# Dense layer with seven products: sums on VectorE, another PSUM bank for the second part, a later fourth part, three buffers for narrowed weights

## Chip, cores and metric

The kernel runs on one core of a Trainium2 chip. The metric is the device time of one execution in microseconds (us); three executions of the kernel before are shown.

## What is computed

The reference has three stages: an attention whose weights are sigmoids, an expert layer with one of eight experts per token, and a dense layer. The change touches the dense layer and the weights that are prepared for it. It is, for 1792 tokens, `d_model` 768 and `d_ff` 2048:

```python
def _moe2_ref(x, w_in, w_out) -> np.ndarray:
    h = x @ w_in
    alpha = 1.0
    g = np.where(h > 0.0, h, alpha * (np.exp(np.minimum(h, 0.0)) - 1.0))
    return (g @ w_out).astype(np.float32)
```

The inputs are float32 numbers (`w_in` and `w_out` arrive in a wide form, two words for each number, and are narrowed in the kernel).

## The kernel before

**Products.** Each float32 operand is split in a high part, the operand rounded by a copy on ACT (L1440 for weights), and a low part, the difference, on DVE (L1441). A product is three matmuls: high by high, high by low, low by high.

**Blocks.** The 1792 tokens are 14 tiles of 128; the dense layer takes them in blocks of 4, 4, 4 and 2 tiles. The hidden width is 16 columns of tiles (`f`). For each `f`, *up* makes `x @ w_in`, `curve` makes `g` from it (ACT Relu L1496 and Exp L1497, DVE `m` L1498, then the split into `gh` L1501 on ACT and `gl` L1502 on DVE), and *down* multiplies `g` by the rows of `w_out` and adds to the accumulators (L1519, six matmuls for each token tile). The downs of a step are run in the step after it (`pend`).

**Block 0** runs up as 18 matmuls of 128x512 (L1487 to L1489) and narrows the weights beside it: `narrow_wide` reads one wide weight (load at L148) in two halves, ACT takes the magnitude into `nrw` (L156), DVE makes the number from it (L153 to L173), and SP stores it to device memory (L1578), from where the later blocks load their weights (`refill`, L1417 to L1426). `nrw` is a tile with one buffer, for the weights that block 0 itself does not keep.

**Blocks 1 and 2** take two `f` at a time, a pair `p` from 0 to 7, in `pair_step`. There the up product is cut in halves of the contraction, of the tokens and of the two `f`, and made from seven half products in place of eight. A half product is a *part*: nine matmuls of 128x256 (L1540, L1543, L1544). Its operands are sums and differences: those of the weights are made by `sums` (L1463 to L1466, on GpSimd, called POOL in the profile) and split by `split_sums`; those of the tokens by `plain` (L1395, GpSimd, after the halves at L1387 and L1388). Two PSUM banks, X and Y, hold the parts; ACT and DVE read each half of a bank as it is done and add the parts to `h` (L1599 is the first such addition, L1619 the last copy).

In a step the parts come in the order 0, 1, 3, 6, 2, 5, 4, then most downs. In the pair steps `p` 3 to 6 of block 1 (3 and 4 of block 2) `columns_in` also transposes rows of the next block (L145) into X and Y, from where ACT copies them (L1376; L1382 for the last block); `mixed` makes halves of them in steps 5 and 7 of block 1. In the first steps of a block `finish` copies the results of the block before out of PSUM.

**Order.** PE, ACT and DVE run their instructions in the order in which the code writes them. POOL and SP are ordered by the framework. A PSUM bank is waited for as a whole.

In the code below `X` and `Y` are the tiles `acc_1907` and `acc_1908`; `xl`, `xr` and `yl`, `yr` their left and right halves.

Of the kernel before, what the change touches and what calls it, by code (L numbers as in the profile page):

```python
# [12 lines left out]
F32 = mybir.dt.float32  # L13
# [10 lines left out]
P = 128  # L24
B, H, S, D = 4, 12, 448, 64
DM = H * D
# [19 lines left out]
HT = TB * P // 2  # L46
# [48 lines left out]
def build(nc, tc, a):  # L95
    q, k, v, k_left, v_left, consts = (a[n] for n in ("q", "k", "v", "k_left", "v_left", "consts"))
    wg, w1, w2, wi, wo, out = a["wg"], a["w1"], a["w2"], a["wi"], a["wo"], a["out"]
    wide = [w[f].bitcast(I32) for f in range(KF2) for w in (wi, wo)]
    with ExitStack() as top:
# [80 lines left out]
        with ExitStack() as st:  # L180
# [500 lines left out]
            nxt = None  # L681
            for n in range(steps + 1):
# [13 lines left out]
                if p == 0 and n < steps:  # L696
                    if n:
                        cur = nxt
                    if T + 1 < steps // 2:
                        nxt = split_tiles(nxt_raw)  # L700
                        if T + 2 < steps // 2:
                            nxt_raw = load(*divmod(T + 2, 3))
                    else:
                        nxt = None
# [9 lines left out]
                for c in range(4):  # L714
# [16 lines left out]
                    if hp == 1 and b > 0 and c in (2, 3):  # L731
                        m = min(4, b * S // P - done_lgt)
# [62 lines left out]
            fv, s1, slot_i = rt([NTT], "fv"), rt([NTT], "s1"), rt([NTT], "slot_i", I32)  # L795
# [514 lines left out]
        with ExitStack() as st:  # L1310
# [7 lines left out]
            b0p = firsts.enter_context(  # L1318
                tc.tile_pool(name="b0p", reuse_waits="tile", bufs=1, side="right")
            )  # L1320
# [6 lines left out]
            seven = [0 < bi and nt == TB for bi, (_, nt) in enumerate(blocks)]  # L1327
# [33 lines left out]
            def rows_in(bi, k):  # L1361
                t0, nt = blocks[bi]
                if 0 <= k < nt:
                    rows_of(t0 + turn_of(bi, k), rows_tile(k))

            def columns_in(bi, k, g, nxt, bank):

                if not 0 <= k < blocks[bi][1]:
                    return
                t, r = turn_of(bi, k), rows_tile(k)  # L1370
                pt = bank.rearrange("p (c n) -> p c n", c=4)[:, :3]
                for j in range(3):
                    cc = 3 * g + j
                    flip(pt[:, j], r[:, cc * P : (cc + 1) * P])
                if seven[bi]:
                    nc.scalar.copy(xr_t[bi > 1][:, 2 * (t // 2) + g], pt)  # L1376
                    if (t // 2, g) == (1, 1):
                        plain(bi, nxt, t % 2)
                    return
                xh, xl = nxt  # L1380
                o = (slice(None), slice(3 * g, 3 * g + 3), slice(t * P, (t + 1) * P))
                nc.scalar.copy(xh[o], pt)  # L1382
                nc.vector.tensor_sub(xl[o], pt, xh[o])
# [6 lines left out]
            def plain(bi, nxt, t):  # L1390
                r = xr_t[bi > 1]
                halves_in(nxt, slice(0, 2), r[:, :2], t)
                halves_in(nxt, slice(2, 3), r[:, 3:], t)
                for o, m, n in ((0, 2, 0), (2, 3, 2), (3, 3, 0), (1, 1, 3)):
                    nc.gpsimd.tensor_sub(r[:, o], r[:, m], r[:, n])  # L1395

            def mixed(bi, nxt, t):
                r = xr_t[bi > 1]
# [56 lines left out]
            def split_out(bi, f):  # L1455
                pair = [wsp.tile([P, DM], F32R, name=n) for n in ("woh", "wol")]
                split(pair, held[1].pop((bi, f)))
                return pair

            def sums(bi, p):  # L1460
                r, r2 = (raw_in(bi, 2 * p + j) for j in range(2))
                (s1, s2), (s4, s3) = ((s[:, 0], s[:, 1]) for s in sraw)
                nc.gpsimd.tensor_add(s1, r2[:, :3], r2[:, 3:])  # L1463
                nc.gpsimd.tensor_sub(s2, s1, r[:, :3])
                nc.gpsimd.tensor_sub(s4, r[:, 3:], s2)
                nc.gpsimd.tensor_sub(s3, r[:, :3], r2[:, :3])  # L1466

            def split_first(bi, p):
                split(a1, raw_in(bi, 2 * p))
# [22 lines left out]
            def curve(n, ph):  # L1492
                m = gp.tile([P, TB * P], F32, name="m", bufs=1)
                gh = gp.tile([P, TB * P], F32R, name="gh")
                gl = gp.tile([P, TB * P], F32R, name="gl")
                nc.scalar.activation(m[:, :n], ph[:, :n], AF.Relu, scale=-1.0)  # L1496
                nc.scalar.activation(m[:, :n], m[:, :n], AF.Exp, scale=-1.0)  # L1497
                nc.vector.scalar_tensor_tensor(  # L1498
                    m[:, :n], m[:, :n], -1.0, ph[:, :n], op0=ALU.add, op1=ALU.max
                )  # L1500
                nc.scalar.copy(gh[:, :n], m[:, :n])  # L1501
                nc.vector.tensor_sub(gl[:, :n], m[:, :n], gh[:, :n])  # L1502
                return gh, gl
# [27 lines left out]
            def run_down(some):  # L1531
                for d in some:
                    down(*d)

            def part(o, w, x, i, start=False):

                (ah, al), (xh, xl) = w, x
                for cc in range(3):
                    a, b, c = ah[:, cc], xh[:, i, cc], xl[:, i, cc]
                    nc.tensor.matmul(  # L1540
                        o, a, b, start=(start and cc == 0), stop=False, skip_group_check=True
                    )
                    nc.tensor.matmul(o, a, c, start=False, stop=False, skip_group_check=True)  # L1543
                    nc.tensor.matmul(  # L1544
                        o, al[:, cc], b, start=False, stop=(cc == 2), skip_group_check=True
                    )
# [16 lines left out]
            def narrow_wide(i, h):  # L1563
                f, k = divmod(i, 2)
                part_ = halves_of[h]
                if h == 0:
                    if f < DIRECT:
                        narrow_to[0] = b0p.tile([P, DM], F32, name="nrw")
                    else:
                        key, narrow_to[0] = claim(k)  # L1570
                        assert key == (0, f)
                dst = narrow_to[0]
                for _ in narrow(dst[:, part_], cv_w[:, part_], cv_t[:, 0, part_], cv_t[:, 1, part_], True):
                    pass
                if i + 1 < 2 * KF2:
                    wide_load(cv_w[:, part_], i + 1, part_)
                if h:
                    nc.sync.dma_start(stored[k][f], dst)  # L1578
                    kept_of[k].add(f)
# [4 lines left out]
            def pair_step(bi, p, x, pend, nxt):  # L1584
                n = TB * P
                after = following(bi, p)
                later_ = following(*after)
                pairs = seven[after[0]]
                X, Y = acc_t[:2]
                xl, yl, yr = X[:, :HT], Y[:, :HT], Y[:, HT:]  # L1590
                h = [gp.tile([P, n], F32, name=f"h{j}", bufs=1) for j in range(2)]
                p1, u2, p5 = (gp.tile([P, HT], F32, name=m, bufs=1) for m in ("p1", "u2", "p5"))
                wa, wb = ([w[:, o] for w in a1] for o in (slice(0, 3), slice(3, 6)))
                w_s = [[s[:, j] for s in ss] for j in range(4)]
                rows_in(bi + 1, p - 2)
                part(xl, wa, x, 0, True)
                nc.scalar.copy(p1, xl)
                part(yr, wb, x, 1, True)
                nc.vector.tensor_add(h[0][:, :HT], yr, p1)  # L1599
                if pairs:  # L1600
                    split_first(*after)
                    w_next = None
                else:
                    w_next = split_in(*after)
                part(yl, w_s[0], x, 3, True)
                nc.scalar.copy(p5, yl)
                part(xl, w_s[1], x, 6)
                nc.scalar.copy(u2, xl)
                if pairs:
                    split_sums(0)  # L1610
                part(yl, w_s[2], x, 2)
                nc.vector.tensor_add(h[0][:, HT:], yl, u2)
                part(xl, w_s[3], x, 5)
                nc.vector.tensor_add(h[1][:, HT:], xl, p5)
                if pairs:
                    split_sums(1)
                run_down(pend[:1])
                part(xl, a2, x, 4)
                nc.scalar.copy(h[1][:, :HT], xl)  # L1619
                if pairs:  # L1620
                    split_last(*after)
                    if seven[later_[0]]:
                        sums(*later_)
                g0 = curve(n, h[0])
                run_down(pend[1:4])
                k = p - 3
                if seven[bi + 1] and p in (5, 7):
                    mixed(bi + 1, nxt, (p - 5) // 2)
                columns_in(bi + 1, k, 0, nxt, Y)
                w20 = split_out(bi, 2 * p)  # L1630
                g1 = curve(n, h[1])
                run_down(pend[4:6])
                columns_in(bi + 1, k, 1, nxt, X)
                run_down(pend[6:])
                w21 = split_out(bi, 2 * p + 1)
                refill()
                return tiles_of(bi, 2 * p, g0, w20) + tiles_of(bi, 2 * p + 1, g1, w21), w_next
# [112 lines left out]
```

## Time and profile before

| | us |
|---|---|
| three executions | 944.29, 944.78, 947.71 |
| median | 944.78 |
| profiled execution | 948.97 |
| its span in the trace | 946.9 |
| PE busy in the span | 877.8 (93%) |
| DVE busy | 641.6 (68%) |
| ACT busy | 526.3 (56%) |
| POOL busy | 180.8 (19%) |

The span is what the trace covers; the profiled execution's own time holds a little more. The mean clock that was granted to PE is 0.978 of full speed. The dense layer's block 0 begins a little ahead of 412 us, its pair steps at 567 us, and its last block at some 860 us.

### The profile page before, as it was taken

What the parts mean: (1) busy time and instruction counts of PE and PEld (TensorE: products, weight loads), DVE (VectorE), ACT (ScalarE), POOL (GpSimd) and SP (SyncE); (2) the same over time, 40 slices, a digit from 0 to 9 for tenths busy, and PEclk for the clock granted to TensorE, in tenths of its full rate; (3) what the DMA queues carried; (4) which work ended last, traced back from release to release, by engine and by line L of the source; (5) the groups of instructions that cost most, each with busy time, mean ns of one, the idle gap of its engine ahead of it and who ended that gap; (6) DMA issues with size and microseconds to landing.
All of it is one profiled execution on the core that took longest, in us unless ns stands there. A gap on an engine that the chain in (4) does not pass through costs nothing.

```text
span 946.9 us, 15423 instructions
## 1 busy us (share of the span) xinstructions
PE 877.8 (93%) x5620; PEld 731.6 (77%) x5620; DVE 641.6 (68%) x956; ACT 526.3 (56%) x796; POOL 180.8 (19%) x159
## 2 busy tenths in 40 slices
PE   9999999999998989898899976999889898999998
PEld 6444555999987779786678766888788888889997
DVE  4878786975664559865578887566666665664664
ACT  7777865544454548643355545456556455564664
POOL 1000001122100123510002053342443322400100
PEclk9999999999999999999999988899999999999999
DMA  8899967899562679476464652423232423232740
GB/s 306 276 317 312 314 215 275 287 400 346 187 210 91 231 282 399 130 278 189 143 190 122 226 174 96 151 81 121 84 117 67 145 89 100 68 101 89 245 152 33
DMA packets 64203, 180.83 MB, mean 191 GB/s; under 512 B 8010, under 2 KB 12234, under 8 KB 64098
## 3 DMA queue, kind: packets, MB, share of 16 engines
q1 hardware_dynamic: 59474, 160.27, 50.1%
q0 software_dynamic: 4480, 19.01, 5.8%
q8 instruction: 59, 0.97, 0.4%
q14 instruction: 46, 0.38, 0.1%
q10 hardware_dynamic: 144, 0.20, 0.1%
HBM read 152.58 MB, written 29.89 MB: 193 GB/s over the span
## 4 chain that ended last, share of the span: by engine, by line
PE 29%; DVE 14%; ACT 8%; issue 4%; DMA 3%; SPq 0%; ACTq 0%; DVEq 0%
PE acc L1519 6%; PE pt L1519 5%; PE acc L1540 5%; PE acc L1544 4%; PE acc L1543 4%; DVE m L1498 3%; DVE wol L1441 2%; ACT woh L1440 2%; PE acc L1487 2%; PE acc L1489 2%; PE acc L1488 2%; DVE raw L165 1%; DMA wi_d<-nrw 1%; ACT gh L1501 1%; DMA wor<-wo_d 1%
## 5 line engine op out<-in xcount | busy, mean ns | idle before, releaser
L594 DVE TENSOR_TENSOR wlo<-raw,whi 128x1536 fp32r<-128x1536 f32 x64 | 111.5, 1760 | 31.8 <-ACT whi L592 29.4
L253 ACT ACTIVATE at<-ps,bias 128x896 f32<-128x896 f32 x96 | 82.5, 916 | 39.1 <-PE ps L300 35.4
L592 ACT CAST whi<-raw 128x1536 fp32r<-128x1536 f32 x64 | 93.7, 1480 | 15.4 <-PE acc L603 9.6
L1519 PE MATMUL acc<-wol,gh 128*128 128x256 f32 x320 | 102.1, 319 | 0.0
L1519 PE MATMUL acc<-woh,gh 128*128 128x256 f32 x320 | 102.1, 319 | 0.0
L1519 PE MATMUL acc<-woh,gl 128*128 128x256 f32 x320 | 101.6, 317 | 0.0
L601 PE MATMUL acc<-whi,both 128*128 128x384 f32 (+1 forms) x236 | 85.1, 361 | 4.3 <-issue 2.8
L602 PE MATMUL acc<-wlo,both 128*128 128x384 f32 (+1 forms) x236 | 83.6, 354 | 0.6 <-DVE wlo L594 0.6
L603 PE MATMUL acc<-whi,both 128*128 128x384 f32 (+1 forms) x236 | 83.3, 353 | 0.0
L1540 PE MATMUL acc<-x,ss 128*128 128x256 f32 x192 | 60.0, 313 | 23.9 <-DVE h L1599 23.9
L1501 ACT CAST gh<-m 128x512 fp32r<-128x512 f32 (+1 forms) x64 | 36.3, 567 | 78.6 <-DVE m L1498 78.6
L1441 DVE TENSOR_TENSOR wol<-wor,woh 128x768 fp32r<-128x768 f32 x64 | 64.5, 1008 | 11.6 <-ACT woh L1440 10.3
L1502 DVE TENSOR_TENSOR gl<-m,gh 128x512 fp32r<-128x512 f32 (+1 forms) x64 | 42.7, 667 | 40.5 <-ACT gh L1501 40.5
L1519 PEld LDWEIGHTS acc<-woh,gh 128*128 128x128 f32 x320 | 61.4, 192 | 10.3
L1519 PEld LDWEIGHTS acc<-wol,gh 128*128 128x128 f32 x320 | 61.2, 191 | 9.5
L1441 DVE TENSOR_TENSOR a<-wir,a 128x768 fp32r<-128x768 f32 (+1 forms) x47 | 50.7, 1078 | 20.4 <-ACT a L1440 20.3
L1519 PEld LDWEIGHTS acc<-woh,gl 128*128 128x128 f32 x320 | 61.0, 191 | 4.4
L1540 PEld LDWEIGHTS acc<-x,ss 128*128 128x128 f32 x192 | 41.2, 215 | 27.1 <-DVE h L1599 27.1
L274 PE MATMUL po<-at,vt 128*64 128x448 f32 (+1 forms) x300 | 59.4, 532 | 1.7 <-DVE xT L305 1.7
L1544 PE MATMUL acc<-x,ss 128*128 128x256 f32 x192 | 58.2, 303 | 0.0
L1519 PE MATMUL pt<-woh,gh 128*128 128x512 f32 x128 | 52.3, 409 | 6.3 <-ACT woh L1440 6.3
L1543 PE MATMUL acc<-x,ss 128*128 128x256 f32 x192 | 58.2, 303 | 0.0
(325 smaller groups left out, 2422.8 us busy)
## 6 DMA issues: line engine op xcount, KB each, us to landing
raw<-in_w SPq DMA_DIRECT2D x132, 384.0 KB
wor<-wo_d SPq DMA_DIRECT2D x60, 384.0 KB
wir<-wi_d SPq DMA_DIRECT2D x58, 384.0 KB
raw<-in_wi SPq DMA_DIRECT2D x9, 768.0 KB
raw<-in_wo SPq DMA_DIRECT2D x9, 768.0 KB
raw<-in_wi SPq DMA_DIRECT2D x14, 384.0 KB
raw<-in_wo SPq DMA_DIRECT2D x14, 384.0 KB
qr<-in_q SPq DMA_DIRECT2D x11, 448.0 KB
```

Source lines behind the costliest of these rows:

```text
L253: nc.scalar.activation(out, ps, AF.Sigmoid, bias=bias, scale=QK_SCALE)
L274: nc.tensor.matmul(po[half(j), o : o + step], vt[0][:, 2 * (n % 2) + j, c, :], at[:, 2 * c + j, o : o + step], start=(c == o == 0), stop=F ...
L592: nc.scalar.copy(w_hi, raw)
L594: nc.vector.tensor_sub(w_lo, raw, w_hi)
L601: nc.tensor.matmul(o, a_hi, b_hi, start=first, stop=False)
L602: nc.tensor.matmul(o, a_hi, b_lo, start=False, stop=False)
L603: nc.tensor.matmul(o, a_lo, b_hi, start=False, stop=last)
L1441: nc.vector.tensor_sub(pair[1], raw, pair[0])
L1519: nc.tensor.matmul(o, a, b, start=(clears and f == 0 and k_ == 0), stop=(f == KF2 - 1 and k_ == 2), skip_group_check=True,)
L1540: nc.tensor.matmul(o, a, b, start=(start and cc == 0), stop=False, skip_group_check=True)
L1543: nc.tensor.matmul(o, a, c, start=False, stop=False, skip_group_check=True)
L1544: nc.tensor.matmul(o, al[:, cc], b, start=False, stop=(cc == 2), skip_group_check=True)
```

## The change

Four things are changed. The four instructions of `sums` and those of `plain` are issued on VectorE in place of GpSimd, and `sums` is called later in the step, after the downs, instead of after `split_last`. Part 1 goes to the right half of bank X (`xr`) instead of Y's, and is issued ahead of part 0. Two downs instead of one stand ahead of part 4, and the transposes of `columns_in` are moved ahead of the curve and the split that they followed. `nrw` gets three buffers.

```diff
--- before.py
+++ after.py
@@ -1392,7 +1392,7 @@
                 halves_in(nxt, slice(0, 2), r[:, :2], t)
                 halves_in(nxt, slice(2, 3), r[:, 3:], t)
                 for o, m, n in ((0, 2, 0), (2, 3, 2), (3, 3, 0), (1, 1, 3)):
-                    nc.gpsimd.tensor_sub(r[:, o], r[:, m], r[:, n])
+                    nc.vector.tensor_sub(r[:, o], r[:, m], r[:, n])
 
             def mixed(bi, nxt, t):
                 r = xr_t[bi > 1]
@@ -1460,10 +1460,10 @@
             def sums(bi, p):
                 r, r2 = (raw_in(bi, 2 * p + j) for j in range(2))
                 (s1, s2), (s4, s3) = ((s[:, 0], s[:, 1]) for s in sraw)
-                nc.gpsimd.tensor_add(s1, r2[:, :3], r2[:, 3:])
-                nc.gpsimd.tensor_sub(s2, s1, r[:, :3])
-                nc.gpsimd.tensor_sub(s4, r[:, 3:], s2)
-                nc.gpsimd.tensor_sub(s3, r[:, :3], r2[:, :3])
+                nc.vector.tensor_add(s1, r2[:, :3], r2[:, 3:])
+                nc.vector.tensor_sub(s2, s1, r[:, :3])
+                nc.vector.tensor_sub(s4, r[:, 3:], s2)
+                nc.vector.tensor_sub(s3, r[:, :3], r2[:, :3])
 
             def split_first(bi, p):
                 split(a1, raw_in(bi, 2 * p))
@@ -1565,7 +1565,7 @@
                 part_ = halves_of[h]
                 if h == 0:
                     if f < DIRECT:
-                        narrow_to[0] = b0p.tile([P, DM], F32, name="nrw")
+                        narrow_to[0] = b0p.tile([P, DM], F32, name="nrw", bufs=3)
                     else:
                         key, narrow_to[0] = claim(k)
                         assert key == (0, f)
@@ -1587,16 +1587,16 @@
                 later_ = following(*after)
                 pairs = seven[after[0]]
                 X, Y = acc_t[:2]
-                xl, yl, yr = X[:, :HT], Y[:, :HT], Y[:, HT:]
+                xl, xr, yl = X[:, :HT], X[:, HT:], Y[:, :HT]
                 h = [gp.tile([P, n], F32, name=f"h{j}", bufs=1) for j in range(2)]
                 p1, u2, p5 = (gp.tile([P, HT], F32, name=m, bufs=1) for m in ("p1", "u2", "p5"))
                 wa, wb = ([w[:, o] for w in a1] for o in (slice(0, 3), slice(3, 6)))
                 w_s = [[s[:, j] for s in ss] for j in range(4)]
                 rows_in(bi + 1, p - 2)
+                part(xr, wb, x, 1, True)
                 part(xl, wa, x, 0, True)
                 nc.scalar.copy(p1, xl)
-                part(yr, wb, x, 1, True)
-                nc.vector.tensor_add(h[0][:, :HT], yr, p1)
+                nc.vector.tensor_add(h[0][:, :HT], xr, p1)
                 if pairs:
                     split_first(*after)
                     w_next = None
@@ -1614,24 +1614,23 @@
                 nc.vector.tensor_add(h[1][:, HT:], xl, p5)
                 if pairs:
                     split_sums(1)
-                run_down(pend[:1])
+                run_down(pend[:2])
                 part(xl, a2, x, 4)
                 nc.scalar.copy(h[1][:, :HT], xl)
                 if pairs:
                     split_last(*after)
-                    if seven[later_[0]]:
-                        sums(*later_)
-                g0 = curve(n, h[0])
-                run_down(pend[1:4])
                 k = p - 3
                 if seven[bi + 1] and p in (5, 7):
                     mixed(bi + 1, nxt, (p - 5) // 2)
                 columns_in(bi + 1, k, 0, nxt, Y)
+                g0 = curve(n, h[0])
+                run_down(pend[2:4])
+                columns_in(bi + 1, k, 1, nxt, X)
                 w20 = split_out(bi, 2 * p)
                 g1 = curve(n, h[1])
-                run_down(pend[4:6])
-                columns_in(bi + 1, k, 1, nxt, X)
-                run_down(pend[6:])
+                run_down(pend[4:])
+                if pairs and seven[later_[0]]:
+                    sums(*later_)
                 w21 = split_out(bi, 2 * p + 1)
                 refill()
                 return tiles_of(bi, 2 * p, g0, w20) + tiles_of(bi, 2 * p + 1, g1, w21), w_next
```

On PE, in the second pair step of block 1, parts 1 and 0 (weights `a_11800` and `a_11801`) go to bank X (`acc_1907`), and parts 3 (to `acc_1908`) and 6 (to `acc_1907`) follow with the sums' splits `ss`. A wait for `DVE_49` is a wait for a DVE instruction, here the addition at L1599, one for `Activation_49` for an ACT instruction. First the end of part 1 and the start of part 3:

```order
-L1540 MATMUL acc_1908<-x_12336,a_11800 128x256
-L1543 MATMUL acc_1908<-x_12337,a_11800 128x256
-L1544 MATMUL acc_1908<-x_12336,a_11801 128x256
-L1540 MATMUL acc_1908<-x_12336,ss_11804 128x256 [waits DVE_49]
+L1540 MATMUL acc_1907<-x_12336,a_11800 128x256
+L1543 MATMUL acc_1907<-x_12337,a_11800 128x256
+L1544 MATMUL acc_1907<-x_12336,a_11801 128x256
+L1540 MATMUL acc_1908<-x_12336,ss_11804 128x256
 L1543 MATMUL acc_1908<-x_12337,ss_11804 128x256
 L1544 MATMUL acc_1908<-x_12336,ss_11805 128x256
```

The wait for DVE has left part 3. It stands at the start of part 6, 18 rows further on in the same step:

```order
 L1543 MATMUL acc_1908<-x_12337,ss_11804 128x256
 L1544 MATMUL acc_1908<-x_12336,ss_11805 128x256
-L1540 MATMUL acc_1907<-x_12336,ss_11804 128x256 [waits Activation_49]
+L1540 MATMUL acc_1907<-x_12336,ss_11804 128x256 [waits DVE_49]
 L1543 MATMUL acc_1907<-x_12337,ss_11804 128x256
 L1544 MATMUL acc_1907<-x_12336,ss_11805 128x256
```

So the product that waits for L1599 is the next one that writes bank X. On DVE, between the end of the first pair step and the start of the second, the rows from the last `m` on (`wi_1827` and `sraw` hold the sums, `wir` is a raw weight):

```order
 L1498 SCALAR_TENSOR_TENSOR m<-m,h_13030 128x512
 L1502 TENSOR_TENSOR gl<-m,gh 128x512
-L1441 TENSOR_TENSOR wol<-wor,woh 128x768
-L1599 TENSOR_TENSOR h_13184<-acc_1908,p_13186 128x256
+L1463 TENSOR_TENSOR wi_1827<-wir 128x384
+L1464 TENSOR_TENSOR wi_1827<-wi_1827,wir 128x384
+L1465 TENSOR_TENSOR sraw<-wir,wi_1827 128x384
+L1466 TENSOR_TENSOR sraw<-wir 128x384
+L1441 TENSOR_TENSOR wol<-wor,woh 128x768
+L1599 TENSOR_TENSOR h_13184<-acc_1907,p_13186 128x256
 L1441 TENSOR_TENSOR a_11801<-wir,a_11800 128x768
 L1441 TENSOR_TENSOR ss_11805<-wi_1827,ss_11804 128x768
```

The four sums stand ahead of the last split of the step and of the addition. On ACT, in block 0, the first half of the second weight that goes to `nrw` (`raw_120` is the wide weight; `DMAHW..` are semaphores of transfers):

```order
-L156 ACTIVATE nrw<-raw_120 128x384 [waits DMAHW6_49,DMAHW1_49,DVE_49]
-L1496 ACTIVATE m<-acc_1908 128x512 [waits PE_49,Activation_49]
+L156 ACTIVATE nrw<-raw_120 128x384 [waits DMAHW6_49]
+L1496 ACTIVATE m<-acc_1908 128x512 [waits DVE_49,PE_49]
 L1497 ACTIVATE m<-m 128x512 [waits Activation_49]
 L1501 CAST gh<-m 128x512 [waits DVE_49]
 L1440 CAST woh<-wor 128x768 [waits DMAHW7_49]
```

The narrowing on ACT has one wait for a transfer in place of two and one for DVE, and the curve stands behind it as before.

## Rows read from the trace of the kernel before

**Rows 1.** Stretches: start:end and length, busy us (count) per engine, PEclk, DMA share, GB/s.
```profile
412.00:567.00 155.00, 136.87 (x656) 111.47 (x654) 116.92 (x210) 72.07 (x123) 23.49 (x20) 0.97 0.59 190
567.00:852.00 285.00, 255.60 (x1695) 235.91 (x1695) 182.15 (x220) 155.43 (x274) 92.69 (x77) 0.95 0.33 102
```

**Rows 2.** Waits, 405 to 567 us: engine, line <- releaser: us, times, longest.
```profile
ACT nrw L156 <- DMA wi_d<-nrw: 18.9, 3, 6.7
ACT nrw L156 <- DMA wo_d<-nrw: 12.8, 2, 6.5
PE pt L1519 <- ACT woh L1440: 6.3, 4, 2.5
PE acc L1487 <- DVE m L1498: 5.8, 4, 2.5
PE acc L1540 <- DVE m L1498: 3.7, 1, 3.7
```

**Rows 3.** Timeline of PE, starts of up products in block 0: start, us, operation, idle before.
```profile
420.71 0.40 PE L1487 MATMUL acc<-both,a 128*128 128x512 f32 x1
429.12 0.40 PE L1487 MATMUL acc<-both,ss 128*128 128x512 f32 x1
486.56 0.50 PE L1487 MATMUL acc<-both,a 128*128 128x512 f32 x1 [0.99 <-DVE m L1498]
495.39 0.39 PE L1487 MATMUL acc<-both,ss 128*128 128x512 f32 x1
504.12 0.39 PE L1487 MATMUL acc<-both,a 128*128 128x512 f32 x1
```

**Rows 4.** Waits, 570 to 720 us (block 1's pair steps).
```profile
PE acc L1540 <- DVE h L1599: 14.2, 8, 6.3
```

**Rows 5.** Timeline of PE, starts of part 3 in six of the pair steps.
```profile
572.64 0.39 PE L1540 MATMUL acc<-x,ss 128*128 128x256 f32 x1 [1.98 <-DVE h L1599]
665.34 0.52 PE L1540 MATMUL acc<-x,ss 128*128 128x256 f32 x1 [1.80 <-DVE h L1599]
725.37 0.39 PE L1540 MATMUL acc<-x,ss 128*128 128x256 f32 x1 [1.73 <-DVE h L1599]
819.14 0.39 PE L1540 MATMUL acc<-x,ss 128*128 128x256 f32 x1 [0.59 <-DVE h L1599]
835.64 0.39 PE L1540 MATMUL acc<-x,ss 128*128 128x256 f32 x1 [0.59 <-DVE h L1599]
852.14 0.39 PE L1540 MATMUL acc<-x,ss 128*128 128x256 f32 x1 [0.59 <-DVE h L1599]
```

**Rows 6.** Groups of POOL, 440 to 947 us: shapes, count, busy us, mean ns, idle before.
```profile
L1464 POOL TENSOR_TENSOR wi<-wi,wir 128x384 f32<-128x384 f32 x16 | 24.7, 1544 | 1.2
```

**Rows 7.** Timelines of DVE and ACT in the last two plain steps, 826 to 850 us.
```profile
827.84 1.50 DVE L1498 SCALAR_TENSOR_TENSOR m<-m,h 128x512 f32<-128x512 f32 x1
...
839.15 0.96 DVE L1441 TENSOR_TENSOR ss<-wi,ss 128x768 fp32r<-128x768 f32 x1 [2.35 <-ACT ss L1440]
840.03 0.42 DVE L1612 TENSOR_TENSOR h<-acc,u 128x256 f32<-128x256 f32 x1
...
842.19 0.37 ACT L1619 COPY h<-acc 128x256 f32<-128x256 f32 x1 [1.36 <-PE acc L1544]
...
844.20 0.69 DVE L1498 SCALAR_TENSOR_TENSOR m<-m,h 128x512 f32<-128x512 f32 x1 [0.64 <-ACT m L1497]
...
849.01 0.69 DVE L1502 TENSOR_TENSOR gl<-m,gh 128x512 fp32r<-128x512 f32 x1 [0.69 <-ACT gh L1501]
```

**Rows 8.** Groups of DVE over the whole span, by shape.
```profile
L1388 DVE TENSOR_TENSOR x<-xr,x 128x384 fp32r<-128x384 f32 x2 | 1.1, 551 | 0.0
L1110 DVE SCALAR_TENSOR_TENSOR xg<-acc,slot_gate,xg 128x384 f32<-128x384 f32 x24 | 14.1, 614 | 19.0 <-PE acc L1109 11.7 <-PE acc L603 7.2
```

**Rows 9.** Stretches behind two starts of part 3, columns as in rows 1.
```profile
665.60:668.70 3.10, 3.10 (x16) 3.10 (x16) 1.01 (x1) 0.37 (x1) 2.80 (x3) 0.50 0.66 209
725.50:728.50 3.00, 3.00 (x27) 3.00 (x28) 0.68 (x1) 1.15 (x3) 0.00 (x0) 1.00 0.70 190
```

## The prediction

> **What bounds the kernel now.** I read the table of stretches first [rows 1], since a change that gives VectorE (DVE) more work can only pay where TensorE (PE) stands still. In 412 to 567 us (most of block 0) PE is busy for 136.9 of 155.0 us, in 567 to 852 us (block 0's last `down`s and 15 pair steps) for 255.6 of 285.0. So 18 and 29 us are idle, and the change touches both stretches. The waits say what ends them, and it differs.
>
> In block 0 [rows 2] a chain, not a busy engine, holds PE. ScalarE (ACT) stood 18.9 us (three times) and 12.8 us (twice) until the store of `nrw` had ended, because that tile has one buffer and the next weight is narrowed into it. Behind that wait lie ACT's part of the curve and its copy of the next weights, and PE waited 5.8 us for `m` and 6.3 us for `woh`. The price is read from the starts of the up products [rows 3]: 420.71 to 429.12 is 8.41 us with no wait, and 429.12 to 486.56, five steps with the store's waits, is 57.44, 11.5 each. With column transposes in it, a step without waits takes 8.73 (495.39 to 504.12).
>
> In the pair steps part 3's first product can't start before DVE's addition at L1599: eight waits of 14.2 us in block 1 alone [rows 4]. Of the starts of part 3 [rows 5] the two last steps, 819.14 to 835.64 and 835.64 to 852.14, are plain ones, 16.50 us each with 0.59 idle. PE's own work in one is 15.91.
>
> **Part one, three buffers for `nrw`.** The order shows the narrowing's wait for the last store gone and that for a load left. The five steps then take 4 x 8.41 + 8.73 = 42.4 us against 57.44, a gain of 15.1. What PE's slow clock costs behind the long waits lies in the 57.44 and goes too. Next late is the load of the raw weight, on a DMA share of 0.59 here [rows 1]. Bounds: 57.44 - 5 x 8.41 = 15.4 above, half of 15.1 below, if that load takes the store's place. I take 15.1, near the undisturbed rows.
>
> **Part two, the sums and `plain` leave GpSimd.** While GpSimd works, at 1.54 us for its longest sum [rows 6], DVE is slowed: `m` takes 1.50 us at 827.84, beside the sums, and 0.69 at 844.20 with GpSimd still [rows 7]. The Trainium skill, SBUF — State Buffer, section "Who interferes with whom", has the rule: VectorE operations with two inputs in SBUF and GpSimd operations that read SBUF lock each other out for a whole instruction. The rows agree; by that rule alone the move could only gain, and the time would be that of rival (a) below. The loop that follows is why I don't take it so.
>
> No sum runs on DVE before. Nearest rows [rows 8]: L1388, a subtraction of 128x384 in SBUF too, 551 ns; above it L1110, 128x384 with one operand more, 614 ns. Below: an operation of 0.96 us at 839.15 lets the next start after 0.88 [rows 7], so 0.08 overlap, and 0.47 is the least. Two of the four sums wait for the one before them and can't overlap (0.59 with the step between, estimated), two can: 2 x 0.59 + 2 x 0.47 = 2.12 us a set, with bounds of 1.9 and 2.5. In 14 of 15 pair steps they now stand on DVE between the last `gl` and the last `wol`, ahead of the addition that PE waits for.
> At block 0's end `plain` and two sets of sums are added to DVE (2.1 each), but nothing stretches it there any more; PE stood 3.7 us for `m` in one wait and up to 2.5 in others [rows 2]. I take a gain of 4.4 of these 6.2 (bounds 0 and 6.2).
>
> **Part three, the second part opens bank X, the fourth comes later.** By the order, DVE's wait leaves part 3's first product and stands at part 6's, the next that writes bank X. Between them lie nine products, 1.05 us. The Trainium skill, PSUM — Partial Sum Buffer, section "PSUM bank collisions raise a hardware error", says to guard PSUM by bank and not by address. The order's wait agrees (the reader holds the right half, the writer the left); with a guard by address no product of the step would wait, and the time would again be rival (a)'s.
>
> So what is moved is a place in a loop, whose length I add up from the last plain step [rows 5, 7]. Before: part 3 (835.64) to the copy at L1619 (842.19) 6.55; to the start of the last `gl` (849.01) 6.82. After: the first becomes 6.55 - 1.05, which now lies ahead of the wait, + 1.04 for the `down` that now comes ahead of part 4, 6.54. Then 6.82; `gl` to the first sum 0.61 (0.69 less the overlap); the sums 2.12; `wol` 0.88; the addition 0.42; and 0.06 to PE. That is 17.4 us, against 16.50 before and PE's 15.91. Bank and later part together give the loop nothing, the sums lengthen it: a plain step gets 0.9 us **longer** and waits 1.5 us at part 6.
>
> The 15 steps by what else they hold: five plain ones 17.4 (87.0); three with columns for the next block, 0.6 allowed for the copy that joins, 18.0 (54.0); two with `plain`, whose halves and subtractions (0.96 + 0.55 + 2.1) now lie in the same chain, 21.1 (42.2); two with `mixed` halves, 2.1 and 1.5 allowed, 19.5 and 18.9; the two first ones of a block, with the finish of the last, 19.3 and 19.9; the last one has no sums, 15.9. That is 276.7 us, against 852.14 - 572.64 = 279.5 before [rows 5].
>
> The 279.5 holds slow clock, the 276.7 doesn't. Behind an idle of 1.80 us (665.34) the granted clock was 0.50, which is 1.2 GHz; behind 1.73 (725.37) it was full [rows 5, 9]. At 0.50 there were 16 products in 3.1 us, at 1.00 27 in 3.0: a loss of 1.3 us, and the slow stretch may go beyond it, so I take 1.7. The light steps' 1.5 stays under 1.73. Seven starts come behind a heavy step (the two with `plain`, the two with `mixed`, the two with a finish, and block 0's end) and wait longer: 7 x 1.7 = 11.9. The pair steps lose 276.7 + 11.9 - 279.5 = 9.1 us.
>
> **Sum:** -15.1 - 4.4 + 9.1 = -10.4 us. The profiled execution took 948.97 us (span 946.9); the median of three timed runs is 944.78, 4.2 below it. All durations are the profiled execution's, which would come to 938.6; from the median the forecast is 944.78 - 10.4 = **934.4 us**.
>
> **The rivals.** (a) The sums cost the loop nothing: no bank waits, or DVE fits them into waits it has anyway. Then the eight light steps lose their 1.5 and six heavy ones 2.1: 8 x 1.5 + 6 x 2.1 = 24.6, 910 us. For it: VectorE stands still for more than a third of the stretch (182 of 285 us busy [rows 1]), and one product type moved off the wait. Against it: the order puts all four sums ahead of the addition, and part 6 waits for it. Chance 0.11.
> (b) Slower: a light step's wait comes to the 1.80 us behind which the clock fell. It takes 0.3 us more in the loop: sums at L1110's 0.61 that don't overlap are 2.46, 0.34 more. Then 14 x 0.34 = 4.8, and eight more steps at 1.7 of slow clock, 13.6: 934.4 + 18.4 = 952.8 us. For it: the margin is thin, and 1.73 and 1.80 are single rows. Against: L1388 is the same kind of operation at 551 ns. Chance 0.11.
> (c) The third buffer swaps one wait for another: the raw weight's load shares SP's queue and the DMA engines with stores and refills, and now it is what the narrowing waits for. Half of 15.1 is lost: 942.0 us. For it: DMA moves 190 GB/s here [rows 1]. Against: its share of 0.59 leaves room. Chance 0.08.
> The forecast keeps 0.70. Its own range is 925 to 945: sums at 1.9 to 2.5 a set are -3 to +5, block 0's end -2 to +4, five of the slow stretches more or fewer 8.
>
> **How the numbers follow.** About 0.5%, 4.7 us, can be told from no change here: below 940.1 is faster, above 949.5 slower. Faster: 0.57 of the forecast's 0.70, (a)'s 0.11 and 0.02 of (c), 0.70. Same: 0.12 of the forecast, 0.06 of (c) and 0.02 of (b), 0.20. Slower: 0.01 and 0.09 of (b), 0.10. The range is 918 to 950: it leaves out nearly all of (a) and most of (b), 0.2 together.
>
> **What would show it.** Right: ACT's waits for `wi_d<-nrw` and `wo_d<-nrw` are gone, up products start every 8.4 to 8.8 us from 420 on, and the pair steps begin some 19 us earlier; `m` takes 0.69 throughout; L1463 to L1466 are on DVE at about 550 ns; part 6 and no longer part 3 waits for L1599, some 1.5 us in a plain step; the 15 pair steps take about 289 us. Wrong: plain steps of 16 us without a wait are (a); a clock of 0.50 behind plain steps' waits is (b); ACT waiting for `raw<-in_wi` or `raw<-in_wo` is (c). If the loop is the wrong one, PE's wait names another releaser than L1599.

## The result, and the profile after

The changed kernel takes 938.84 us (median of 10 executions, 934.85 to 939.93); the kernel before, over 10 executions, 946.64. The ratio is 0.9912 with a 95% interval from 0.9889 to 0.9936: **faster by 0.9%**, 6 to 10.5 us. The profiled execution took 939.29 us, its span 937.5, against 948.97 and 946.9. The forecast was 934.4 us, 10.4 below the median of the three executions it had; the two medians differ by 7.8 us, the two profiled executions by 9.7.

The stretches of the kernel after, with the columns of [rows 1]; the pair steps begin at 546.2 now:

```profile
412.00:546.20 134.20, 128.42 (x650) 106.93 (x648) 112.65 (x222) 71.56 (x121) 6.62 (x6) 1.00 0.67 218
546.20:852.00 305.80, 265.41 (x1763) 246.50 (x1764) 187.98 (x293) 155.83 (x279) 10.49 (x10) 0.94 0.31 97
```

In block 0 PE's idle went from 18 us to 6. In the pair steps it rose, from 29 us of 285 to 40 of 306. The change won in one place and lost in the other. The timeline of PE after shows how much: up products in block 0, the first product of the pair steps, and the first up product of the last block:

```profile
419.39 0.39 PE L1487 MATMUL acc<-both,a 128*128 128x512 f32 x1
427.78 0.39 PE L1487 MATMUL acc<-both,ss 128*128 128x512 f32 x1
470.06 0.39 PE L1487 MATMUL acc<-both,a 128*128 128x512 f32 x1
478.78 0.39 PE L1487 MATMUL acc<-both,ss 128*128 128x512 f32 x1
546.29 0.39 PE L1540 MATMUL acc<-x,a 128*128 128x256 f32 x1 [3.42 <-DVE m L1498]
856.41 0.28 PE L1487 MATMUL acc<-x,a 128*128 128x256 f32 x1
```

And the two that answer to the last two in the kernel before:

```profile
566.99 0.58 PE L1540 MATMUL acc<-x,a 128*128 128x256 f32 x1 [3.74 <-DVE m L1498]
865.79 0.28 PE L1487 MATMUL acc<-x,a 128*128 128x256 f32 x1
```

The starts that answer to [rows 3] are 8.39 and 8.72 us apart; five steps lie between 427.78 and 470.06, 42.28 us where it was 57.44. From the up start at 420.71 (now 419.39) to the first part it was 146.28 us and is 126.90, 19.4 less. From there to the last block it was 298.80 and is 310.12, 11.3 more. The difference of 9.4 between the spans is these two and 1.3 us ahead of 420. Those 1.3 us are no part of the change: over the profiled kernels, the experiments' too, this start lies anywhere between 416.47 and 420.73. Without them the traces differ by 8.1 us, close to the 7.8 of the medians.

Waits after: on ACT in 405 to 546 us, and on PE in 550 to 860 us (where block 1's alone were [rows 4]).

```profile
ACT nrw L156 <- DMA raw<-in_wo: 2.0, 2, 1.6
ACT nrw L156 <- DMA raw<-in_wi: 1.4, 1, 1.4
...
PE acc L1540 <- DVE h L1599: 40.3, 15, 7.4
```

ACT's 31.7 us for the store are gone, and 3.4 us for loads came. PE's wait for L1599, over both blocks 23.9 us before, is 40.3. It stands at part 6 now. Of the prediction's 15 steps eight are light, the plain ones (only the pair itself) and those with columns; six are heavy, with a finish, `plain` or `mixed` in them; the last has no sums. Here are starts of part 6 in plain steps and one with columns (774.51 to 792.57):

```profile
592.32 0.38 PE L1540 MATMUL acc<-x,ss 128*128 128x256 f32 x1 [1.40 <-DVE h L1599]
609.92 0.38 PE L1540 MATMUL acc<-x,ss 128*128 128x256 f32 x1 [1.39 <-DVE h L1599]
...
757.09 0.38 PE L1540 MATMUL acc<-x,ss 128*128 128x256 f32 x1 [1.55 <-DVE h L1599]
774.51 0.38 PE L1540 MATMUL acc<-x,ss 128*128 128x256 f32 x1 [1.55 <-DVE h L1599]
792.57 0.39 PE L1540 MATMUL acc<-x,ss 128*128 128x256 f32 x1 [1.52 <-DVE h L1599]
```

The plain step from 757.09 takes 17.42 us, where [rows 5] had 16.50. DVE's timeline in a step after, from the last `gl` to the addition, shows what fills it:

```profile
806.55 0.69 DVE L1502 TENSOR_TENSOR gl<-m,gh 128x512 fp32r<-128x512 f32 x1 [0.69 <-ACT gh L1501]
807.16 0.55 DVE L1463 TENSOR_TENSOR wi<-wir 128x384 f32<-128x384 f32 x1
807.74 0.56 DVE L1464 TENSOR_TENSOR wi<-wi,wir 128x384 f32<-128x384 f32 x1
808.34 0.56 DVE L1465 TENSOR_TENSOR sraw<-wir,wi 128x384 f32<-128x384 f32 x1
808.81 0.55 DVE L1466 TENSOR_TENSOR sraw<-wir 128x384 f32<-128x384 f32 x1
809.28 0.95 DVE L1441 TENSOR_TENSOR wol<-wor,woh 128x768 fp32r<-128x768 f32 x1
810.15 0.41 DVE L1599 TENSOR_TENSOR h<-acc,p 128x256 f32<-128x256 f32 x1
```

From the first sum to `wol` is 2.12 us, the four taking 0.58, 0.60, 0.47 and 0.47 from start to start, and no idle stands in the chain behind `gl`.

### The profile page after: what moved, and what is told of

It reads as the page before. It is cut to its first block, busy times and chain, and to the rows that moved or that the text cites. A ratio compares the mean times of both kernels' runs of the same rounds, so it can differ in the third digit from the quotient of the medians.

```text
span 937.5 us, 15343 instructions
## 1 busy us (share of the span) xinstructions
PE 869.8 (93%) x5620; PEld 728.5 (78%) x5620; DVE 641.2 (68%) x1036; ACT 524.6 (56%) x796; POOL 82.2 (9%) x79
## 3 DMA queue, kind: packets, MB, share of 16 engines
q0 software_dynamic: 4480, 19.01, 5.9%
## 4 chain that ended last, share of the span: by engine, by line
PE 33%; DVE 12%; ACT 9%; issue 3%; DVEq 0%; ACTq 0%
PE acc L1519 7%; PE pt L1519 7%; PE acc L1540 3%; PE acc L1544 3%; PE acc L1543 3%; PE acc L1487 3%; PE acc L1489 3%; PE acc L1488 3%; DVE m L1498 2%; DVE wol L1441 2%; ACT m L1497 2%; ACT gh L1501 2%; ACT m L1496 2%; ACT woh L1440 1%; DVE wi L1464 1%
## 5 line engine op out<-in xcount | busy, mean ns | idle before, releaser
L592 ACT CAST whi<-raw 128x1536 fp32r<-128x1536 f32 x64 | 93.7, 1480 | 15.4 <-PE acc L603 9.0
L1540 PE MATMUL acc<-x,ss 128*128 128x256 f32 x192 | 61.6, 321 | 40.3 <-DVE h L1599 40.3
L1540 PEld LDWEIGHTS acc<-x,ss 128*128 128x128 f32 x192 | 42.4, 221 | 43.4 <-DVE h L1599 43.3
L1502 DVE TENSOR_TENSOR gl<-m,gh 128x512 fp32r<-128x512 f32 (+1 forms) x64 | 40.0, 626 | 40.5 <-ACT gh L1501 39.8
L1441 DVE TENSOR_TENSOR wol<-wor,woh 128x768 fp32r<-128x768 f32 x64 | 61.0, 954 | 7.9 <-ACT woh L1440 7.1
L1441 DVE TENSOR_TENSOR a<-wir,a 128x768 fp32r<-128x768 f32 (+1 forms) x47 | 38.4, 817 | 37.3 <-ACT a L1440 36.7
L1543 PE MATMUL acc<-x,ss 128*128 128x256 f32 x192 | 59.2, 308 | 0.0
L1544 PE MATMUL acc<-x,ss 128*128 128x256 f32 x192 | 59.0, 307 | 0.0
L1440 ACT CAST woh<-wor 128x768 fp32r<-128x768 f32 x64 | 53.3, 833 | 2.8 <-PE acc L1519 2.8
```

The source lines that it names most:

```text
L592: nc.scalar.copy(w_hi, raw)
L1440: nc.scalar.copy(pair[0], raw)
L1441: nc.vector.tensor_sub(pair[1], raw, pair[0])
L1540: nc.tensor.matmul(o, a, b, start=(start and cc == 0), stop=False, skip_group_check=True)
L1544: nc.tensor.matmul(o, al[:, cc], b, start=False, stop=(cc == 2), skip_group_check=True)
```

## The experiments

Each was timed beside the kernel before, which took 945.35 to 946.98 us there; ratios are to that. Differences from the changed kernel are between medians of separate sessions, so 1 or 2 us in them mean nothing. The theory is the forecast's loop: part 6 (or 3), part 4's copy, two curves, the last split, the addition, and back. The rivals stand in each expectation.

**Only the buffers.** In the kernel before:

```diff
-                        narrow_to[0] = b0p.tile([P, DM], F32, name="nrw")
+                        narrow_to[0] = b0p.tile([P, DM], F32, name="nrw", bufs=3)
```

> The kernel before with nothing but three buffers for nrw. The forecast's theory: ACT's waits for the stores of nrw are the whole of what the five slow up steps of block 0 lose, so up products start every 8.4 to 8.8 us between 420 and 487 us, and the time falls by about 15 us, to a ratio near 0.984 of the kernel before. The rest of block 0's gain (4.4 us) belongs to the move of plain and of the sums and stays away. Rival: the load of the raw weight takes the store's place, ACT waits for raw<-in_wi or raw<-in_wo, and only some 7.5 us are gained (ratio near 0.992). Another rival: the move from GpSimd is what cured block 0, and the time hardly moves (within 3 us).

Measured: 929.97 us against 945.35, 15.4 less, ratio 0.9837 (0.9809 to 0.9865). Its up starts on PE, and the first product of the pair steps:

```profile
428.92 0.39 PE L1487 MATMUL acc<-both,ss 128*128 128x512 f32 x1
471.20 0.39 PE L1487 MATMUL acc<-both,a 128*128 128x512 f32 x1
...
551.46 0.39 PE L1540 MATMUL acc<-x,a 128*128 128x256 f32 x1 [3.51 <-DVE m L1498]
```

The five steps take 42.28 us. This one edit beats the whole change by some 9 us, so the other three together, as they stand, cost time. From its up start at 420.54 to the first part it is 130.92 us, 4.0 more than in the changed kernel: that is what moving `plain` and sums off GpSimd is worth at block 0's end. The next experiment, which differs from the changed kernel in the engine alone, confirms it: 130.97 us there (419.79 to 550.76).

**Sums and `plain` on GpSimd, at their new places.** In the changed kernel `nc.vector` becomes `nc.gpsimd` in all of `sums` and in `plain`'s subtraction:

```diff
-                nc.vector.tensor_add(s1, r2[:, :3], r2[:, 3:])
+                nc.gpsimd.tensor_add(s1, r2[:, :3], r2[:, 3:])
...
-                    nc.vector.tensor_sub(r[:, o], r[:, m], r[:, n])
+                    nc.gpsimd.tensor_sub(r[:, o], r[:, m], r[:, n])
```

> The changed kernel with the sums and plain issued on GpSimd again, at their new places in the code. The forecast's theory: the four sums on DVE make the loop of a plain pair step 17.4 us; without them the loop is about 16.1 (0.8 us of it m's stretching beside GpSimd), so a plain step takes 16.0 to 16.5 us and part 6 waits under 0.6 us there; the heavy steps gain 1 to 2 us each; block 0's end loses some 4 us again. Sum: 5 to 12 us faster than the changed kernel, 927 to 934 us on its median of 938.8. Rival: GpSimd's slowing of DVE costs the loop as much as the sums do on DVE, the plain steps stay at 17 us or more, and with block 0's 4 us the kernel is slower than the changed one (940 to 945).

Measured: 912.5 us, 0.9654 (0.9629 to 0.9678), 26 us below the changed kernel. The direction is the theory's, the size isn't. It had GpSimd stretch the first `m` inside the loop, as in [rows 7]. POOL's and DVE's timelines of this kernel in a plain step show it stretch something else, mostly the split of `a`:

```profile
792.77 1.02 POOL L1466 TENSOR_TENSOR sraw<-wir 128x384 f32<-128x384 f32 x1
...
792.84 1.37 DVE L1441 TENSOR_TENSOR a<-wir,a 128x384 fp32r<-128x384 f32 x1 [1.99 <-ACT a L1440]
794.13 0.68 DVE L1498 SCALAR_TENSOR_TENSOR m<-m,h 128x512 f32<-128x512 f32 x1
```

The later part 4 lets the last sum end (793.79) before `m` starts; the split of `a` takes 1.37 us (0.56 in the changed kernel), while ACT is still at its exponentials. A step from first part to first part (790.78 to 806.55) takes 15.77 us: PE's own work, which the prediction's subtraction put at 15.91. The heavy steps gained more than the expected 1 to 2 us as well, three in a row 4.4, 4.3 and 3.3 (in the changed kernel from the first parts at 664.55, 687.15 and 710.40): slow clock came at four starts instead of seven. The kernel is also 17 us below the one with the buffers alone. So the bank, the later part 4 and the earlier transposes together gain time; with the sums on DVE ahead of the addition the whole loses it.

**Sums on DVE, but outside the loop.** In the changed kernel, `sums` is called in the next step behind L1599:

```diff
                 nc.vector.tensor_add(h[0][:, :HT], xr, p1)
                 if pairs:
+                    if (bi, p) != (1, 0):
+                        sums(*after)
                     split_first(*after)
...
-                if pairs and seven[later_[0]]:
-                    sums(*later_)
```

> The changed kernel with the sums still on DVE, but called in the next step, just behind the addition at L1599 and ahead of split_first's subtraction, which is outside the loop from part 6 back to itself. The forecast's theory: the loop of a plain step is then 15.3 us, shorter than PE's own 15.9, so plain steps take 15.9 to 16.1 us with waits under 0.4 us, heavy ones lose 2.1 us, and fewer starts come at half clock: 22 to 30 us faster than the changed kernel, 909 to 917 us. Rival: the sums only move their wait. They now stand ahead of the splits of a and ss on DVE, PE then waits for those at the start of a later part, and a plain step stays at 17 us or more (935 to 942 us).

Measured: 906.46 us, 0.9584 (0.9557 to 0.961): 32 us below the changed kernel with the same operations on the same engine. Its first parts of two steps on PE, and its waits:

```profile
801.53 0.28 PE L1540 MATMUL acc<-x,a 128*128 128x256 f32 x1
817.30 0.28 PE L1540 MATMUL acc<-x,a 128*128 128x256 f32 x1
...
PE acc L1540 <- DVE h L1599: 15.3, 7, 5.4
```

That is a little below the expected 909 to 917. A plain step takes 15.77 us and doesn't wait; seven waits are left of fifteen, and slow clock comes at four starts instead of seven. This is the theory's clearest test: neither the engine nor the work cost the 32 us, but the place ahead of the addition.

**One sum twice.** In the changed kernel the last sum is issued again in each step, to the same tile (four lines are added, so L1540 and L1599 are L1544 and L1603):

```diff
                 if pairs and seven[later_[0]]:
                     sums(*later_)
+                    again(*later_)
...
+            def again(bi, p):
+                r, r2 = (raw_in(bi, 2 * p + j) for j in range(2))
+                nc.vector.tensor_sub(sraw[1][:, 1], r[:, :3], r2[:, :3])
```

> The changed kernel with the last of the four sums issued twice in every pair step, to the same tile, so that what is computed is the same. The forecast's theory: the loop of every pair step with sums grows by 0.47 to 0.55 us, and part 6 waits 2.0 us in a plain step, more than the 1.80 us behind which the clock fell before: granted clock 0.50 behind plain steps' waits, 14 x 0.5 = 7 us of DVE and up to 8 x 1.7 = 13.6 us of clock, 15 to 21 us slower than the changed kernel (954 to 960 us). Rival: the clock doesn't hang on a wait of that length, the stretches behind plain steps stay at 1.00, and only the 7 us are lost (945 to 947). Second rival: DVE has slack there and nothing changes (within 2 us).

Measured: 955.24 us, 1.0108 (1.0083 to 1.0132), 16.4 us above the changed kernel and slower than the kernel before. Starts of part 6 on PE, and the stretches behind the first two:

```profile
763.31 0.39 PE L1544 MATMUL acc<-x,ss 128*128 128x256 f32 x1 [2.16 <-DVE h L1603]
781.35 0.39 PE L1544 MATMUL acc<-x,ss 128*128 128x256 f32 x1 [2.16 <-DVE h L1603]
801.63 0.39 PE L1544 MATMUL acc<-x,ss 128*128 128x256 f32 x1 [2.11 <-DVE h L1603]
...
763.51:766.51 3.00, 3.00 (x28) 3.00 (x28) 1.32 (x2) 1.11 (x2) 0.00 (x0) 1.00 0.73 202
781.55:784.55 3.00, 3.00 (x18) 3.00 (x18) 1.07 (x2) 1.10 (x2) 0.00 (x0) 0.62 0.77 188
```

18.04 us from 763.31, and 20.28 from 781.35 (a step with columns, 18.06 in the changed kernel): of the eight waits behind light steps (1.97 to 2.16 us) five were followed by a clock below 1.00. So rival (b)'s mechanism exists, though not every such wait sets it off: of two waits of 2.16 us one did and one didn't. The changed kernel's waits behind light steps, 1.37 to 1.55 us, are half a microsecond shorter, and none was followed by slow clock.

**The bank, with the sums out.** From the third experiment's kernel, part 1 goes back to Y:

```diff
-                xl, xr, yl = X[:, :HT], X[:, HT:], Y[:, :HT]
+                xl, yl, yr = X[:, :HT], Y[:, :HT], Y[:, HT:]
...
-                part(xr, wb, x, 1, True)
                 part(xl, wa, x, 0, True)
                 nc.scalar.copy(p1, xl)
-                nc.vector.tensor_add(h[0][:, :HT], xr, p1)
+                part(yr, wb, x, 1, True)
+                nc.vector.tensor_add(h[0][:, :HT], yr, p1)
```

> The kernel with the sums behind L1599 (e3_sums_behind_h), with part 0 first and part 1 in the right half of bank Y, as before the change. The forecast's theory: the bank moves the wait by one part, 1.05 us, and nothing else. The addition then stands right between part 1 and part 3, so even a step that PE bounds shows the 0.59 us of idle of the kernel before: about 0.7 us in each light step, 1.05 in each heavy one, 10 to 14 us slower than e3's 906.5 (917 to 921). Rival: with the sums out of the loop the bank makes no difference (within 3 us of 906.5).

Measured: 927.58 us, 0.9801 (0.9761 to 0.9842), 21 us above the third. The start of part 3 on PE:

```profile
800.15 0.38 PE L1540 MATMUL acc<-x,ss 128*128 128x256 f32 x1 [0.59 <-DVE h L1599]
816.61 0.38 PE L1540 MATMUL acc<-x,ss 128*128 128x256 f32 x1 [0.59 <-DVE h L1599]
```

The plain step (16.46 us, with its 0.59) is as the theory has it. The surplus over 10 to 14 lies in the heavy steps, whose waits, 2.06 to 3.71 us in the five of them from 647 to 731 us, brought slow clock five times; at the same five starts the third experiment's kernel had it twice.

**One down, and `plain` outside.** From the third experiment's kernel again, one down ahead of part 4 (first piece), `plain`'s subtractions put off to the next step (second piece), and both:

```diff
-                run_down(pend[:2])
+                run_down(pend[:1])
...
-                run_down(pend[2:4])
+                run_down(pend[1:4])
```

```diff
                     split_first(*after)
+                    while left:
+                        differences(left.pop())
```

(`left` holds what `plain` has put off, `differences` are its four subtractions.)

> e3_sums_behind_h with one down ahead of part 4 instead of two, as before the change. The forecast's theory: the second down lies in the loop, 1.04 us; plain steps, which PE bounds in e3, don't change, the six steps that still wait in e3 (5.41, 2.64, 1.29, 2.63, 1.04 and 1.83 us) lose up to 1.04 each: 4 to 8 us faster, 899 to 903. Rival: the second down covers DVE's addition that part 4 waits for (the last one of the four); with one down PE waits there and the time stays or rises by up to 5 us.

> e3_sums_behind_h with plain's four subtractions (block 2's tokens only) put off to the next pair step, behind L1599 and split_first's subtraction. The forecast's theory: they are the rest of DVE's work in the loop of the two steps with plain; PE's waits of 2.64 and 2.63 us behind those fall to about 0.3, and one stretch at half clock goes: 4.6 to 6.5 us faster than e3, 900 to 902. Rival: behind L1599 they delay the split of ss, for which a later part waits, and the time stays within 2 us of 906.5.

> The edits of e6_one_down_ahead and e7_plain_behind_h together. The forecast's theory: the gains overlap in the two steps with plain, so 7 to 11 us faster than e3 (896 to 900). Rival as in e6: a wait at part 4 takes the place, and it is no faster than e7 alone.

Measured: 903.85 us, 0.9544 (0.9502 to 0.9586); 903.88 us, 0.9564 (0.9521 to 0.9607); 905.13 us, 0.9567 (0.9529 to 0.9605). All three lie above their expected ranges, none can be told apart from the third experiment's 906.46, and the two edits don't add up. The waits name the reason, first those of PE's weight loads (PEld) with one down ahead (two lines added), then those of PE with `plain` outside (eight added to the first addition's line, twelve to the later one's):

```profile
PEld acc L1540 <- DVE h L1616: 3.1, 12, 0.3
...
PE acc L1548 <- DVE h L1607: 12.2, 7, 5.4
...
PE acc L1548 <- DVE h L1626: 2.4, 2, 1.2
```

With one down ahead, PE's waits for the first addition fell from 15.3 to 10.5 us, but part 4's weight load waits up to 0.3 us for the last addition before it, in twelve steps, and a plain step (774.42 to 790.59) takes 16.17 us in place of 15.77. With `plain` outside, the waits for the first addition fell by 3.1 us, and two new ones of 1.2 came for that later one, which the moved subtractions delay. With both edits these two are 2.2 each. So the second down does cover that addition, as the sixth experiment's rival had it.

**The old place, the bank and the down in the changed kernel itself.** Three edits of the changed kernel, one each: `sums` behind `split_last`; parts 0 and 1 as in the bank's experiment; `run_down(pend[:1])` and `[1:4]`.

```diff
                     split_last(*after)
+                    if seven[later_[0]]:
+                        sums(*later_)
...
-                if pairs and seven[later_[0]]:
-                    sums(*later_)
```

> The changed kernel with the four sums on DVE, but called where they stood before the change, right behind split_last and ahead of the first curve. The forecast's theory: that place lies in the loop too, between the copy at L1619 and the first m; DVE waits about 0.64 us for ACT there anyway, so 0.5 to 0.6 of the 2.12 us are hidden, a plain step takes 16.8 to 16.9 us, and the kernel is 6 to 12 us faster than the changed one (927 to 933). Rival: the place matters for the engine's wait alone and is out of the loop, plain steps at 15.9 us, 910 us or less.

> The changed kernel with part 0 first and part 1 in the right half of bank Y, as before the change, two downs still ahead of part 4. The forecast's theory: the wait goes back to part 3, the loop of a step gets longer by 1.05 us (18.4 to 18.5 in a plain step), and the wait of 2.5 us brings half clock to most plain steps: 14 x 1.05 = 15 us and 4 to 14 us of clock, 957 to 968 us. Rival: the bank is worth the 0.59 of idle alone, 8 us, 945 to 949.

> The changed kernel with one down ahead of part 4, as before the change. The forecast's theory: the loop is 1.04 us shorter, 16.4 us in a plain step with 0.5 us of wait, and heavy steps lose the same, with one or two fewer stretches at half clock: 14 to 20 us faster than the changed kernel, 919 to 925. Rival: part 4 then waits for DVE's last addition (L1614), and half of that is lost, 929 to 933.

Measured: 926.44 us, 0.9796 (0.976 to 0.9832); 966.9 us, 1.0214 (1.0178 to 1.025); 921.97 us, 0.9744 (0.971 to 0.9778). PE's starts of part 6 (part 3 in the second) in a plain step of each:

```profile
745.56 0.38 PE L1540 MATMUL acc<-x,ss 128*128 128x256 f32 x1 [0.97 <-DVE h L1599]
762.40 0.39 PE L1540 MATMUL acc<-x,ss 128*128 128x256 f32 x1 [0.97 <-DVE h L1599]
```
```profile
773.34 0.38 PE L1540 MATMUL acc<-x,ss 128*128 128x256 f32 x1 [2.57 <-DVE h L1599]
791.78 0.38 PE L1540 MATMUL acc<-x,ss 128*128 128x256 f32 x1 [2.58 <-DVE h L1599]
```
```profile
742.97 0.38 PE L1540 MATMUL acc<-x,ss 128*128 128x256 f32 x1 [0.52 <-DVE h L1599]
759.35 0.38 PE L1540 MATMUL acc<-x,ss 128*128 128x256 f32 x1 [0.51 <-DVE h L1599]
```

Steps of 16.84, 18.44 and 16.38 us, where 16.8 to 16.9, 18.4 to 18.5 and 16.4 were expected. The times lie in the expected ranges too, the first 0.6 us below its own. The earlier transposes were not tried by themselves.

## Why the prediction was right, and where it was off

**Part one** held: 15.1 us forecast, 15.4 measured by itself. Of rival (c) three waits came, 3.4 us in all, but the five steps took 42.28 us where 42.4 stood, so they cost PE nothing.

**Part two, block 0's end**: 4.4 forecast, 4.0 from the traces of the first two experiments. DVE's `m` of 128x512 is 0.69 us in the mean, without stretching.

**Part two, the price of the sums, and part three, the loop**: 2.12 us a set, as forecast; 17.42 us for a plain step in block 2 (17.4), 18.06 for one with columns (18.0), a wait of 1.37 to 1.55 (1.5) at part 6. That the sums lengthen the loop is what most of the forecast hung on, and taking them out of it gave 32 us, moving the bank back cost 28, taking a down out gave 17, slow clock included. Rival (a) didn't come true in the changed kernel; the 910 us that it would give are about what the kernels without sums in the loop take.

**The size of the pair steps' loss** was a bit too small: 9.1 forecast, 11.3 measured from the first part to the last block. The 15 steps, from part 6 at 552.86 to part 6 at 843.79, took 290.9 us, where 276.7 and 11.9 stood. The light steps are right within 0.3 us, so the mis-sized terms are the heavy ones and the slow clock. That came at seven starts, as counted, but 1.7 us for each was low for some: the step from 572.27 (7.40 of idle before it, and 15 products in 3 us behind it) to 592.32 takes 20.05 us, the next plain one at full clock 17.60, so 2.4. For others it was right: the plain step from 738.08 to 757.09, at slow clock too, takes 19.01 against 17.42, so 1.6. A step with `plain` at full clock (628.16 to 649.65) is 21.49, where 21.1 stood:

```profile
572.27 0.58 PE L1540 MATMUL acc<-x,ss 128*128 128x256 f32 x1 [7.40 <-DVE h L1599]
...
628.16 0.38 PE L1540 MATMUL acc<-x,ss 128*128 128x256 f32 x1 [1.37 <-DVE h L1599]
649.65 0.58 PE L1540 MATMUL acc<-x,ss 128*128 128x256 f32 x1 [4.61 <-DVE h L1599]
...
572.47:575.47 3.00, 3.00 (x15) 3.00 (x16) 0.60 (x1) 0.88 (x2) 0.97 (x1) 0.50 0.75 209
```

**The total** is a little off for two reasons. The change gained 7.8 us and not 10.4, for the most part by what the pair steps lost beyond the forecast; and the three executions that the forecast started from had a median 1.9 us below that of the ten.

**One edit had no price.** The sum has no term for the earlier transposes. Before, PE waited 5.7 us in the pair steps for copies of the transposed rows, at a step's first product (3.2 for L1376, 2.5 for L1383); in the changed kernel these waits are gone. What the edit is worth by itself stays open.

**One sentence was too broad**: "Bank and later part together give the loop nothing" holds for the loop's length in the changed kernel, where one takes 1.05 us and the other gives 1.04 back. It hides that the bank also ends the 0.59 us that PE loses in any step bound by itself. With the sums out of the loop the bank is worth 21 us: 0.7 in each light step, the rest in the heavy ones, whose waits it shortens. The second experiment's expectation failed by the same kind of haste: it took GpSimd's stretching of `m` from the order before, though the later part 4 had moved `m` behind the sums.

## What to carry to other kernels

Where one engine waits for another once in every step, add up the loop from that wait back to itself and compare it with the busy engine's own work: an operation put inside the loop lengthens it by its own duration, less what it hides in waits that stand there anyway, and each step pays what then goes beyond the busy engine's work. Here the 2.12 us of sums cost a plain step 1.65 us at the loop's end (17.42 against 15.77) and 1.07 at their old place; a few instructions later, behind the one that releases the wait, they cost it nothing. A bundle of edits can gain because one of them gains more than the rest lose; time the one with the certain mechanism by itself (here the buffers: 15.4 us alone, 8 for the whole).

## What the runs showed of the hardware that wasn't expected

The length of an idle alone doesn't tell whether PE's clock falls behind it. In all these traces the clock stayed full behind idles of 1.55 us and less in the pair steps. But with the bank moved back in the changed kernel two idles of the same 2.48 us were followed by different clocks (first four rows), and in the kernel before, an idle of 2.25 us was followed by full clock (last two):

```profile
596.04 0.39 PE L1540 MATMUL acc<-x,ss 128*128 128x256 f32 x1 [2.48 <-DVE h L1599]
614.73 0.50 PE L1540 MATMUL acc<-x,ss 128*128 128x256 f32 x1 [2.48 <-DVE h L1599]
...
596.24:599.24 3.00, 3.00 (x26) 3.00 (x26) 0.61 (x1) 1.12 (x3) 0.00 (x0) 1.00 0.77 221
614.93:617.93 3.00, 3.00 (x15) 3.00 (x16) 0.61 (x1) 0.37 (x1) 0.00 (x0) 0.50 0.73 212
...
683.80 0.38 PE L1540 MATMUL acc<-x,a 128*128 128x256 f32 x1 [2.25 <-ACT raw L1376]
684.00:687.00 3.00, 2.41 (x19) 2.21 (x19) 1.49 (x4) 1.68 (x3) 0.00 (x0) 1.00 0.28 62
```

Of the two, one granted 1.00 (2.4 GHz), the other 0.50 (1.2 GHz). The prediction took 1.73 and 1.80 for the two sides of a line; that was two rows, and the 2.25 us, in the same trace, already lay on the wrong side. So the prediction's line doesn't hold, though none of the eight waits behind light steps, the longest 1.55 us, was followed by slow clock. What decides behind longer ones was not tried.
